# Three pairs of 128-row TensorE transposes done in 64-row halves, weight loads released by products, and a new order up to the wide gate products

## The chip, the cores and the metric

The kernel runs on one core of a Trainium2 chip. The core has five engines with separate instruction queues: TensorE (PE, matrix products; its weight loads are shown as PEld), VectorE (DVE), ScalarE (ACT), GpSimd (POOL) and SyncE (SP), which here only issues transfers. The metric is the device time of one execution in microseconds (us). Three runs of the kernel before took 202.31, 202.59 and 202.63 us, a median of 202.59.

## What is computed

The input x has 2048 rows of 448 bf16 numbers. Two blocks follow one another, each with a layer norm ahead and a residual sum behind:

```python
qkv = layernorm(x) @ wqkv                       # 16 heads of 28
pq, pk = q @ w_phi, k @ w_phi                   # per head
phi = concat(softmax(p), softmax(-p))           # for p = pq and pk
kv, z = phi_k.T @ v, sum(phi_k)                 # over all 2048 rows
o = (phi_q @ kv) / (phi_q @ z + 1e-6)
h = x + o @ wo
g, u = layernorm(h) @ w_gate, layernorm(h) @ w_up    # 448 -> 1792
out = h + (sigmoid(g) * u) @ w_down
```

## The kernel before, in words

The 2048 rows are 16 tiles of 128 rows, numbered t = 0 to 15, in four chunks of four tiles. A product contracts over the partitions, so each tile must be transposed (features on partitions, rows along the free axis) before it meets a weight. 448 features are held as four blocks of 128 partitions, of which some half blocks are padding; therefore most products are made in pairs of 64 rows: one product uses array rows 0 to 63 and the other rows 64 to 127, at the same time, into two PSUM banks. The helper `both` (L304 to L310) issues such pairs, so nearly all products have line L309. An operation that is split over such pairs has a part "a" and a part "b"; in part "b" the array halves and the banks are swapped, and PE waits between the two for its own part "a".

The stages are these. First x is loaded, normalised (`xn`), and transposed: tiles 0 to 3 by PE against an identity (`pe_transpose`, L533 to L541; the products have line L538 and the copy out of PSUM, `xT0e` and so on, L531), the other twelve tiles by transfers that transpose. For each tile the products `pva`, `pvb` give k and v; ACT makes the two exponentials of k (`ek`, L671 and L672), DVE the row sums and their reciprocals (`ss`, `rs`), DVE or POOL the quotient (`phi`, L685), and PE adds the tile into the 28 by 28 sums of all heads (`kva`, `kvb`, 64 by 58 each). Tiles 0 to 3 are made as `vva`, `vvb` and `ppa`, `ppb`. `w2m1_0` to `w2m1_3` fold `w_phi` into the q weights; `pqa`, `pqb` make q of a chunk, of which ACT takes exponentials (`eq`).

When tile 15 has been added, ACT and DVE bring the sums into `kvz`. Then `num` makes numerators and denominators of a tile, DVE combines them (`rsm`, `qq`, `b`, `c`, `rden`), `o` divides (POOL or DVE, L810), the quotient is transposed (tiles 0 and 1 by PE as `oT0`, `oT1`, the others by transfers), `woa`, `wob` multiply by wo, `h` adds x, and the second layer norm gives `hn`. Tiles 0 and 1 of `hn` are again transposed by PE (`hT0`, `hT1`), the others by transfers. Gate and up products (`ga`, `gb`), the tanh (`sig`, L925), the product (`hh`, L926) and the down products (`dn`, `dp`, `dm`, `dl`) end the work. The gate products of tiles 0 to 3 are 256 wide; those from `ga4_1` on, 512 wide, are the wide gates. They begin at 93.7 us of the span.

The order on every engine is written out: the table `ORDER` names the operations of each engine in sequence, and the name's engine in it also says who does a copy that ACT or DVE could do. The class `Graph` derives the waits from what each operation reads and writes. SP's queue is in order too: a transfer whose data is not ready holds back all that stand behind it. The table `PACE` adds waits that no data needs; before it has one entry, by which `ld_wg1` waits for `kva14`. `wwo` and `wgu` are marks in PE's order at which PE waits for the weights wo, and the gate and up weights, and issues nothing.

## Time and profile before

| what | value |
|---|---|
| median of three runs | 202.59 us |
| the profiled execution | 202.7 us, of which the span is 200.8 us |
| PE busy in the span | 195.5 us (97%), granted clock 1.0 |
| DVE, ACT, POOL busy | 132.0, 89.4, 56.2 us |
| HBM read and written | 8.34 and 1.84 MB |

Times in the views count from the start of the span; 1.9 us of the execution lie outside it. A matmul's shown end is modelled and reaches beyond the start of the next, so the step from one start to the next says what a product costs, and the shown length does not.

### The profile page before, as it was taken

How to read it: one execution, taken by the hardware profiler on the slowest of the kernel's cores; microseconds unless marked ns; L12 is line 12 of the kernel's file. 1: busy time of each engine (PE TensorE's matmuls, PEld its weight loads, DVE VectorE, ACT ScalarE, POOL GpSimd, SP SyncE). 2: the span in 40 equal slices, each digit the busy share in tenths (PEclk: the TensorE clock that was granted, in tenths of full speed). 3: DMA queues.
4: the chain of work that ended last, by engine and by line, in shares of the span. 5: the costliest groups of instructions: out<-in, count | busy, mean ns of one | idle time of the engine just before them, and what ended most of it. 6: DMA issues, size and time to landing. Idle time of an engine off the chain costs nothing.

```text
span 200.8 us, 5854 instructions
## 1 busy us (share of the span) xinstructions
PE 195.5 (97%) x2516; PEld 114.4 (57%) x2516; DVE 132.0 (66%) x308; ACT 89.4 (45%) x174; POOL 56.2 (28%) x95
## 2 busy tenths in 40 slices
PE   7999999999999999999999999999999999999995
PEld 4835556565568778787444444555555555554443
DVE  5999999978888986576569877346332422272224
ACT  2668988898883451434232432324323212222220
POOL 5779948633343207510170110001400000000000
PEclk9999999999999999999999999999999999999999
DMA  6965346749984230360015220020312000004002
GB/s 157 316 140 129 54 83 76 221 144 302 309 206 66 52 57 15 66 82 3 0 29 124 56 42 10 20 58 26 65 38 52 0 3 2 0 3 137 0 3 91
DMA packets 32490, 16.26 MB, mean 81 GB/s; under 512 B 24720, under 2 KB 31568, under 8 KB 32464
## 3 DMA queue, kind: packets, MB, share of 16 engines
q1 hardware_dynamic: 32336, 15.86, 33.7%
q8 instruction: 20, 0.33, 0.7%
q14 instruction: 6, 0.05, 0.1%
q10 hardware_dynamic: 128, 0.03, 0.1%
HBM read 8.34 MB, written 1.84 MB: 51 GB/s over the span
## 4 chain that ended last, share of the span: by engine, by line
PE 92%; ACT 3%; DMA 2%; issue 1%; SPq 1%; DVE 0%
PE psum L309 84%; PE psum L954 5%; DMA wk_sb<-in_A_wqkv_dram 2%; ACT hhT L671 1%; ACT eq L721 1%; ACT hhT L672 1%; PE psum L524 1%; PE psum L538 1%; PE psum L612 1%; SPq L413 1%; PE psum L599 0%; ACT xnT L531 0%; ACT v L531 0%; DVE x_sb L961 0%
## 5 line engine op out<-in xcount | busy, mean ns | idle before, releaser
L309 PE MATMUL psum<-xnT,wu_sb 64*128 64x512 bf16 (+1 forms) x490 | 93.6, 333 | 0.0
L309 PE MATMUL psum<-xnT,wg_sb 64*128 64x512 bf16 (+1 forms) x490 | 93.5, 333 | 0.1
L925 ACT ACTIVATE sg_sb<-psum 128x512 bf16<-128x512 f32 x56 | 33.2, 596 | 90.1 <-PE psum L309 89.5
L926 DVE SCALAR_TENSOR_TENSOR hhT<-sg_sb,psum 128x512 bf16<-128x512 bf16 x56 | 37.7, 684 | 52.1 <-ACT sg_sb L925 51.7
L309 PEld LDWEIGHTS psum<-xnT,wg_sb 64*128 64x128 bf16 x490 | 44.6, 94 | 20.9 <-DVE hhT L926 2.5
L309 PEld LDWEIGHTS psum<-xnT,wu_sb 64*128 64x128 bf16 x490 | 44.7, 94 | 13.9
L309 PE MATMUL psum<-wd_sb,hhT 64*128 64x448 bf16 x336 | 37.3, 349 | 0.0
L309 PEld LDWEIGHTS psum<-wd_sb,hhT 64*128 64x128 bf16 x336 | 17.8, 94 | 14.2 <-DVE x_sb L836 0.5
L309 PE MATMUL psum<-Wk,xnT 64*128 64x448 bf16 x112 | 22.2, 350 | 0.5 <-ACT hhT L672 0.2
L309 PE MATMUL psum<-wv_sb,xnT 64*128 64x448 bf16 x112 | 22.3, 351 | 0.1
L810 POOL TENSOR_TENSOR o_pad<-c_sb,rden 128x448 bf16<-128x448 bf16 x11 | 10.2, 935 | 28.5 <-DVE rden L806 28.4
L675 DVE TENSOR_REDUCE ss<-hhT 128x32 f32<-128x896 bf16 x16 | 16.8, 1060 | 0.2 <-ACT hhT L672 0.2
L721 ACT ACTIVATE eq<-psum 120x1024 bf16<-120x1024 f32 x16 | 15.6, 1030 | 0.6 <-PE psum L309 0.4
L685 POOL TENSOR_TENSOR phi<-hhT,rs 128x896 bf16<-128x896 bf16 x8 | 13.6, 1710 | 5.6 <-DVE rs L681 3.4
L309 PE MATMUL psum<-xnT,Wq 64*120 64x512 bf16 x112 | 14.8, 383 | 0.3 <-ACT eq L721 0.2
L845 POOL TENSOR_SCALAR ve<-ssq 128x1 f32<-128x1 f32 x11 | 2.2, 201 | 41.8 <-ACT junk L842 41.5
L309 PE MATMUL psum<-wo_o,oT 64*128 64x448 bf16 x56 | 13.2, 350 | 0.0
L309 PE MATMUL psum<-wo_e,oT 64*128 64x448 bf16 x56 | 13.2, 349 | 0.0
L961 DVE SCALAR_TENSOR_TENSOR x_sb<-psum,x_sb 128x448 bf16<-128x448 f32 (+2 forms) x17 | 9.4, 592 | 2.9 <-PE psum L954 1.6
L954 PE MATMUL psum<-wd_sb,hhT 128*128 128x448 bf16 (+2 forms) x70 | 11.2, 316 | 0.0
L309 PEld LDWEIGHTS psum<-Wk,xnT 64*128 64x128 bf16 x112 | 7.8, 94 | 5.8 <-PE psum L309 1.0
L671 ACT ACTIVATE hhT<-psum 128x448 bf16<-128x448 f32 x16 | 8.8, 553 | 4.4 <-PE psum L309 4.2
(105 smaller groups left out, 234.4 us busy)
## 6 DMA issues: line engine op xcount, KB each, us to landing
out_dram<-x_sb SPq DMA_DIRECT2D x15, 112.0 KB, 1.8
x_sb<-in_A_x_dram SPq DMA_DIRECT2D x7, 224.0 KB, 4.2
wd_sb<-in_B_w_down_dram SPq DMA_DIRECT2D x7, 224.0 KB, 5.1
wg_sb<-in_B_w_gate_dram SPq DMA_DIRECT2D x3, 448.0 KB, 5.8
wu_sb<-in_B_w_up_dram SPq DMA_DIRECT2D x3, 448.0 KB, 5.7
wv_sb<-in_A_wqkv_dram SPq DMA_DIRECT2D x2, 224.0 KB, 4.7
wk_sb<-in_A_wqkv_dram SPq DMA_DIRECT2D x2, 196.0 KB, 4.1
wo_e<-in_A_wo_dram SPq DMA_DIRECT2D x1, 336.0 KB, 3.3
```

The costliest lines, as they stand in the source:

```text
L309: p = e.matmul(o, lhsT=w, rhs=r, start=st, stop=sp, tile_position=(row, 0))
L413: return op(eng, name, lambda e: e.dma_start(dst, src), r=r, w=w, dma="in" if eng == "sp" else "ain", nring=48 if eng == "sp" else 8, kb=kb)
L671: e.activation(ek[:, s, :, 0, :], src, ACT.Exp)
L675: op("dve", "ss%d" % t, lambda e: e.tensor_reduce(ss[:, s, :].rearrange("p (b h) -> p b h", h=2), eks.rearrange("p b (d h) -> p b h d", h= ...
L685: return e.tensor_tensor(phi[:, sp, :, :, :].rearrange("p b a n -> p (b a) n")[:, :, 0:56].rearrange("p b (d h) -> p b d h", h=2), eks.rea ...
L721: op("act", "eq%d_%d%s" % (c, i, "pm"[sg]), lambda e, sg=sg: e.activation(eq[c][:, sg, 2 * i:2 * i + 2, :].rearrange("p g n -> p (g n)"), ...
L810: return e.tensor_tensor(o_pad[:, t % NO, off:off + D].rearrange("p (h d) -> p h d", h=H), c_sb[:, t % NS, :, 0:DH], rden[:, t % NS, :][:, ...
L845: op(("pool", "dve"), "ve%d" % t, lambda e: e.tensor_scalar(ve2[:, t:t + 1], ssq2[:, t:t + 1], 1.0 / D ** 3, EPS, op0=ALU.mult, op1=ALU.ad ...
L925: op("act", "sig" + nm, lambda e: e.activation(sg_sb[:, k, 0:W], bk(bg)[:, 0:W], ACT.Tanh, scale=0.5), r=[B(bg)], w=[("sg", k)])
L926: op("dve", "hh" + nm, lambda e: e.scalar_tensor_tensor(out=dst, in0=sg_sb[:, k, 0:W].rearrange("p (f n) -> p f n", n=N), scalar=1.0, in1= ...
L954: p = e.matmul(bk(b)[:, lo:hi], lhsT=hb[:, ff, TS(t)], rhs=wd_sb[:, ff, lo:hi], start=ff == 0, stop=ff == FT - 1)
L961: op("dve", "fin%d%s" % (t, nm), lambda e: e.scalar_tensor_tensor(out=h_sb[:, t, lo:hi], in0=bk(b)[:, lo:hi], scalar=0.5, in1=h_sb[:, t, l ...
```

## The change

`pe_transpose` made a tile's transpose as four products over all 128 array rows with 128 columns each. For the pairs xT2/xT3, oT0/oT1 and hT0/hT1 a new function makes both tiles' transposes at once, as 16 products over 64 array rows with 64 columns each; the lower half of the rows of both tiles goes to one PSUM bank and the upper half to the other. There are still two copies out of PSUM for a pair, but each holds one half of the rows of both tiles, so a reader of either tile waits for both copies. xT0 and xT1 stay as they were.

```diff
+        def XT(t):
+            return [("xnT", t, 0), ("xnT", t, 1)]
...
+        def pair_transpose(names, srcs, banks, dst, rkeys, wkeys):
+            ps = [bk16(b)[:, 0:512] for b in banks]
+
+            def f(e):
+                for i, tile in enumerate(srcs):
+                    for kt, src in enumerate(tile):
+                        o = slice((i * KT + kt) * 64, (i * KT + kt + 1) * 64)
+                        for h, rows in enumerate((LO, HI)):
+                            p = e.transpose(ps[h][:, o], src[rows], ident[rows, rows], tile_position=(64 * h, 0))
+                return p
+            op("pe", names[0], f, r=["ident"] + rkeys, w=[B(b) for b in banks], rows=64, half={b: h for h, b in enumerate(banks)})
+            for h in range(2):
+                evac(names[h] + "e", dst[h], ps[h].rearrange("p (t k s) -> p t k s", t=2, k=KT), B(banks[h]), [k[h] for k in wkeys])
...
-            if t < 4:
+            if t in (2, 3):
+                if t == 3:
+                    v = xnT[0][:, :, 2 * P:4 * P].rearrange("p k (t h s) -> p h t k s", t=2, h=2)
+                    pair_transpose(("xT2", "xT3"), [[xn_pad[:, u % NX, kt * P:(kt + 1) * P] for kt in range(KT)] for u in (2, 3)], (6, 7),
+                                   [v[:, 0], v[:, 1]], [("xn", 2 % NX), ("xn", 3 % NX)], [XT(2), XT(3)])
+            elif t < 2:
...
-PACE = {"ld_wg1": "kva14"}
+PACE = {"ld_wg0": "pvb14", "ld_wu0": "pvb15", "ld_wg1": "kvb10", "ld_wu1": "kvb11", "ld_wg2": "kvb12", "ld_wu2": "kvb13", "ld_wg3": "kvb14",
+        "ld_wu3": "pqa1_1", "ld_wd0": "num1", "ld_wd2": "pqb1_1"}
```

`otrans` and `htrans` call the new function in the same way, with banks 2 and 3, and 0 and 1.

The order tables of PE, DVE, ACT and POOL are written anew from xT2 up to about `ga4_1`; behind that, from `num13` on, PE's order is the same word for word. SP's order is unchanged. Between engines these move: `xT3e` from ACT to DVE, `v1_13` from DVE to ACT, `nm1_6`, `nm1_8` and `nm1_12` from ACT to POOL, `phi5` from DVE to POOL and `phi8` from POOL to DVE, `o1`, `o4`, `o10` and `o11` from POOL to DVE, `o7` and `o8` from DVE to POOL, and some small operations of the second layer norm of tiles 2 to 9 both ways. `wgu` moves from among the wide gates to ahead of `num5`, and `wwo` from `kvb14` to behind `pqb1_1`.

The order shows this at three places. On ACT, early in the kernel, between the exponentials of tiles 0 and 1 (L671 and L672 twice) and those of tile 2, the kernel before has:

```order
L455 CAST par<-mask 128x2
L671 ACTIVATE hhT<-psum 128x8x56 [waits s_eng_pe]
L672 ACTIVATE hhT<-psum 128x8x56
L531 COPY xnT<-psum 128x4x128 [waits s_eng_pe]
L671 ACTIVATE hhT<-psum 128x8x56
L672 ACTIVATE hhT<-psum 128x8x56
L531 CAST v<-psum 128x16x28 [waits s_eng_pe]
```

After the change (the same operations stand 1 to 26 lines further down in the file):

```order
L456 CAST par<-mask 128x2
L697 ACTIVATE hhT<-psum 128x8x56 [waits s_eng_pe]
L698 ACTIVATE hhT<-psum 128x8x56
L697 ACTIVATE hhT<-psum 128x8x56
L698 ACTIVATE hhT<-psum 128x8x56
L532 CAST v<-psum 128x16x28 [waits s_eng_pe]
```

The copy of a transposed tile is gone from between the exponentials; it is now a second copy in DVE's queue.

On PE, where the quotients of tiles 0 and 1 are transposed (`o_pad`), between q of chunk 2 and the product with wo, the kernel before has:

```order
L309 MATMUL psum<-xnT,Wq 120x512 [waits s_eng_act]
L309 MATMUL psum<-xnT,Wq 120x512 x7
L538 MATMUL psum<-ident,o_pad 128x128 [waits s_eng_pool,s_eng_dve]
L538 MATMUL psum<-ident,o_pad 128x128 x3
L538 MATMUL psum<-ident,o_pad 128x128 [waits s_eng_pool]
...
L309 MATMUL psum<-kvz,eq 128x60 [waits s_eng_dve]
L309 MATMUL psum<-kvz,eq 128x60 x15
L309 MATMUL psum<-xnT,Wq 120x512 [waits s_eng_pe]
L309 MATMUL psum<-xnT,Wq 120x512 x5
L309 MATMUL psum<-x_sb,ident 128x448 [waits s_eng_dve,s_eng_act]
```

After the change:

```order
L310 MATMUL psum<-xnT,Wq 120x512 [waits s_eng_act]
L310 MATMUL psum<-xnT,Wq 120x512 x7
L548 MATMUL psum<-ident,o_pad 128x64 [waits s_eng_dve,s_eng_pool]
L548 MATMUL psum<-ident,o_pad 128x64 x15
L310 MATMUL psum<-xnT,Wq 120x512 [waits s_eng_pe]
L310 MATMUL psum<-xnT,Wq 120x512 x5
L310 MATMUL psum<-kvz,eq 128x60 [waits s_eng_dve]
L310 MATMUL psum<-kvz,eq 128x60 x15
L310 MATMUL psum<-x_sb,ident 128x448 [waits s_eng_act,s_eng_dve]
```

Two groups of four transposes have become one of sixteen half ones, and the q products (`pqb2_1`) now stand ahead of the 60-column products (`num3`).

On DVE, at the same place, between the numerators of tile 1 and the copy of a transposed quotient out of PSUM, the kernel before has:

```order
L799 TENSOR_TENSOR qq<-rsm,psum 128x16 [waits s_eng_dve]
L801 TENSOR_TENSOR b_sb<-psum,qq 128x464 [waits s_eng_dve]
L804 TENSOR_TENSOR c_sb<-b_sb,psum 128x464 [waits s_eng_dve]
L531 COPY oT<-psum 128x512 [waits s_eng_pe]
L798 RECIPROCAL rsm<-psum 128x16 [waits s_eng_pe]
```

After the change:

```order
L825 TENSOR_TENSOR qq<-rsm,psum 128x16 [waits s_eng_dve]
L836 TENSOR_TENSOR o_pad<-c_sb,rden 128x448 [waits s_eng_dve]
L827 TENSOR_TENSOR b_sb<-psum,qq 128x464 [waits s_eng_dve]
L830 TENSOR_TENSOR c_sb<-b_sb,psum 128x464 [waits s_eng_dve]
L532 COPY oT<-psum 128x8x64 [waits s_eng_pe]
```

The division of tile 1 (`o1`, into `o_pad`) has come into DVE's queue, ahead of tile 2's `b2` and `c2` and of the copy.

34 lines of the change are left out of this document (20 added, 14 removed), and 90 rows, old and new, of the table ORDER.

## The prediction

> **What bounds the kernel now.** I read the busy lines first, then the stretches by stage, then PE's timeline around the three transposes, and last the other engines at the same places.
>
> ```profile
> PE 195.5 (97%) x2516; PEld 114.4 (57%) x2516; DVE 132.0 (66%) x308; ACT 89.4 (45%) x174; POOL 56.2 (28%) x95
> ```
>
> PE is busy nearly all the time, so the end moves only by what leaves PE's queue or by gaps in it. The stretches (length, then busy time of PE, PEld, DVE, ACT, POOL, then granted clock) show where another engine is as full:
>
> ```profile
> 12.00:44.00 32.00, 31.34 (x518) 17.97 (x516) 30.95 (x62) 28.30 (x63) 23.22 (x21) 1.00 0.53 122
> 44.00:59.00 15.00, 14.44 (x255) 8.41 (x249) 12.65 (x37) 13.27 (x19) 5.74 (x7) 1.00 0.97 256
> 59.00:94.00 35.00, 35.00 (x630) 28.40 (x630) 27.21 (x74) 12.65 (x29) 10.31 (x17) 1.00 0.34 58
> 94.00:198.50 104.50, 104.31 (x1012) 52.45 (x1008) 51.65 (x110) 30.11 (x57) 8.98 (x20) 1.00 0.14 34
> ```
>
> From 12 to 44 us DVE is idle 1.05 us of 32, and most of that is one wait at the end: there PE and DVE run neck and neck. From 44 to 59 us a chain of dependent steps leads from the last sum over the rows to the first gate product. Behind 59 us PE has no gap; the order from there on changes only up to 94 us. So the change must earn its time ahead of 59 us, and a saving on PE counts there only where nothing else is late.
>
> PE's timeline at the three places (start, length, what; steps between starts are real, ends are modelled):
>
> ```profile
> 11.23 0.29 PE L524 MATMUL psum<-zero 128*128 128x128 bf16 x2
> 11.35 0.61 PE L538 MATMUL psum<-ident,xn_pad 128*128 128x128 bf16 x8
> 11.89 1.74 PE L309 MATMUL psum<-wv_sb,xnT 64*128 64x448 bf16 x14
> 13.82 1.74 PE L309 MATMUL psum<-Wk,xnT 64*128 64x448 bf16 x14 [0.19 <-ACT hhT L672]
> ...
> 18.02 0.35 PE L309 MATMUL psum<-Wk,xnT 64*128 64x448 bf16 x1 [0.18 <-ACT v L531]
> ...
> 41.34 1.05 PE L309 MATMUL psum<-xnT,Wq 64*120 64x512 bf16 x8
> 42.22 0.39 PE L309 MATMUL psum<-v,phi 64*128 64x58 bf16 x16
> ...
> 49.19 1.07 PE L309 MATMUL psum<-xnT,Wq 64*120 64x512 bf16 x8 [0.25 <-ACT eq L721]
> 50.20 0.62 PE L538 MATMUL psum<-ident,o_pad 128*128 128x128 bf16 x8
> 50.75 0.40 PE L309 MATMUL psum<-kvz,eq 56*128 56x60 bf16 x16
> 50.99 0.84 PE L309 MATMUL psum<-xnT,Wq 64*120 64x512 bf16 x6
> 51.66 0.35 PE L309 MATMUL psum<-x_sb,ident 64*128 64x448 bf16 x2
> ...
> 57.59 0.62 PE L538 MATMUL psum<-ident,hn_pad 128*128 128x128 bf16 x8
> 58.14 0.36 PE L309 MATMUL psum<-wo_e,oT 64*128 64x448 bf16 x1
> 59.01 0.27 PE L309 MATMUL psum<-xnT,wg_sb 64*128 64x256 bf16 x1
> ```
>
> **The transposes on PE.** Eight full transposes take 0.55 us to the next start (50.20 to 50.75; 11.35 to 11.89 and 57.59 to 58.14 likewise). Two warm products of the same 128 columns take 0.12 (11.23 to 11.35), so about 0.07 of the 0.55 is lost at the change from 128-row to 64-row products. Another such loss stands ahead: eight q products take 0.88 (41.34 to 42.22), but 1.01 where transposes follow (49.19 to 50.20), so 0.13. The nearest row for 16 half transposes of 64 columns is the 16 products of 60 columns: 0.24 (50.75 to 50.99). No row shows a half transpose; between 0.24 and 16 times the warm product's 0.06 (0.96) I take 0.24, since rows, columns and pairing are the same. A group then costs PE 0.24 instead of 0.68: 0.44 less at oT, as much at hT, but less at xT, where the warm products ahead keep full rows: 0.54 becomes 0.13 + 0.24 = 0.37, 0.17 less.
>
> [...]
>
> **The front, up to 44 us.** ACT and DVE there:
>
> ```profile
> 12.20 0.59 ACT L531 COPY xnT<-psum 128x512 bf16<-128x512 bf16 x1
> 12.67 0.58 ACT L671 ACTIVATE hhT<-psum 128x448 bf16<-128x448 f32 x1
> 13.10 0.58 ACT L672 ACTIVATE hhT<-psum 128x448 bf16<-128x448 f32 x1
> L531 DVE COPY xnT<-psum 128x512 bf16<-128x512 bf16 x5 | 2.1, 418 | 0.2 <-PE psum L538 0.2
> L531 DVE CAST v<-psum 128x448 bf16<-128x448 f32 x1 | 0.6, 617 | 0.0
> 42.22 1.14 DVE L685 TENSOR_TENSOR phi<-hhT,rs 128x896 bf16<-128x896 bf16 x2
> 44.49 0.81 DVE L750 TENSOR_TENSOR kvz<-psum,mask 64x232 bf16<-64x232 f32 x2 [1.14 <-PE psum L309]
> ```
>
> The copy xT3e leaves ACT: the next exponential starts 0.47 earlier (12.67 - 12.20), and `ppa2`, which waited for it at 13.82, starts at about 13.35, if `vvb0` is through by then: it began its 1.74 at 11.89 and now begins 0.17 earlier. `pva4` at 18.02, which waits for an ACT copy behind the next exponentials, follows by about the same. One fold group (`w2m1_1`) now stands between `ppa2` and `ppb2`, where PE waited anyway. So PE and ACT gain 0.45 early on. DVE takes the copy (0.42) and gives v1_13 away (0.62), 0.20 less by the end of the stage, but 0.42 more until then. Who is last at the end? DVE's last `phi` ends at 43.36 and DVE then idles 1.14 for PE: PE is behind by more than a crossing of halves costs, so PE's gain counts as long as no `phi` comes later than its product. I take 0.45; the ends are 0.20 (only what DVE saves) and 0.80 (PE's gain, and the 0.35 of DVE's idle time beside v1_13). On POOL the three `nm1` and `phi5` for `phi8` come to little; 23.22 busy of 32 hides them. SP's transposing transfers of tiles 4 on wait for POOL's `xn4` behind `nm1_6`, 0.2 later, ahead of products that begin at 18 us.
>
> **oT, 49 to 53.6 us.**
>
> ```profile
> 49.11 0.17 DVE L799 TENSOR_TENSOR qq<-rsm,psum 128x16 f32<-128x16 f32 x1
> 49.31 0.64 DVE L801 TENSOR_TENSOR b_sb<-psum,qq 128x464 bf16<-128x464 f32 x1
> 49.99 0.64 DVE L804 TENSOR_TENSOR c_sb<-b_sb,psum 128x464 bf16<-128x464 bf16 x1
> 50.86 0.42 DVE L531 COPY oT<-psum 128x512 bf16<-128x512 bf16 x1 [0.23 <-PE psum L538]
> L810 DVE TENSOR_TENSOR o_pad<-c_sb,rden 128x448 bf16<-128x448 bf16 x5 | 3.1, 625 | 0.1
> L810 POOL TENSOR_TENSOR o_pad<-c_sb,rden 128x448 bf16<-128x448 bf16 x11 | 10.2, 935 | 28.5 <-DVE rden L806 28.4
> ```
>
> PE saves 0.44, but what it feeds is behind DVE. With `o1` there (0.63, less about 0.08 by which DVE's steps overlap where none waits for the one ahead, as 58.03 + 0.43 and 58.37 below), `b2` starts at 49.86, `c2` at 50.54 and ends at 51.18, and the copy of one half runs from about 51.10 to 51.52. `woa0` follows at about 51.6, against 51.66; PE is ready for it at 51.66 - 0.44 = 51.2 and idles. So of 0.44 only 0.05 arrives; between 0 and 0.44 I take 0.05. POOL is relieved, `o0` alone (0.94) ends in time, and the transfers of oT2 and oT3 behind have until 58.14.
>
> **hT, 53.6 to 59 us.**
>
> ```profile
> 56.83 0.41 DVE L851 TENSOR_SCALAR hn_pad<-x_sb,mv,rst 128x512 bf16<-128x512 bf16 x1
> 58.03 0.43 DVE L531 COPY xnT<-psum 128x512 bf16<-128x512 bf16 x1 [0.15 <-PE psum L538]
> 58.37 0.16 DVE L799 TENSOR_TENSOR qq<-rsm,psum 128x16 f32<-128x16 f32 x1
> 58.44 0.42 DVE L531 COPY xnT<-psum 128x512 bf16<-128x512 bf16 x1
> ```
>
> Again a chain: the second `hn` ends at 57.24 on DVE, and `c4` now stands ahead of both. The transposes can begin at about 57.43 instead of 57.59 and end at 57.67; both copies, 0.8 together, wait for them and for `qq5`, and end at 58.7 instead of 58.86. The first gate product comes at 58.85 instead of 59.01; of these 0.16, 0.05 is oT's, since the chain starts from there, and 0.10 is hT's own out of 0.44. PE idles about 0.4 ahead of it. Bounds 0 and 0.44.
>
> **The weight loads.**
>
> ```profile
> 46.33 0.44 SPq L413 DMA_DIRECT2D wu_sb<-in_B_w_up_dram  x1
> 52.60 2.93 SPq L823 DMA_TRANSPOSE oT<-o_pad  x2
> wu_sb<-in_B_w_up_dram SPq DMA_DIRECT2D x3, 448.0 KB, 5.7
> ```
>
> The last gate or up load was issued at 46.33; now it waits for `pqa1_1`, eight q products (0.88) right behind the last row sums, which DVE's `kvz` follows at 44.49: about 45.4. Those ahead of it go out with the sums of tiles 10 to 14, before nearly all with tile 14. With 5.7 to landing it is there by 51.1, and `wgu` asks shortly before hT's 57.59. SP's oT2 behind the paced loads waits for its quotient until 52.60 anyway. I cost it at nothing; were the cover gone, `num5` and hT would wait for the landing.
>
> **From 59 to 94 us** the same products stand in another order in a stretch without gaps; 0, with 0.2 to either side.
>
> **Sum.** 0.45 + 0.05 + 0.10 = 0.60 off the profiled 202.7 gives 202.1; the median lies 0.11 below that execution, so 202.0.
>
> **The rivals.** *All of PE's savings arrive* (chance 0.13): DVE's order leads `b2` and `c2` in time, and oT and hT count in full: 0.45 + 0.44 + 0.44 = 1.3, 201.3. The idle ahead of `woa0` and of the first gate speaks against it.
>
> *Nothing arrives that can be told* (0.20): DVE's extra 0.42 early on holds the `phi` and with it PE, and only v1_13's 0.20 is won: 202.4.
>
> *The half transposes do not pair* (0.04): 16 steps one after another, each half the warm step, 0.03, make 0.48 a group; the idle at oT and hT hides it, and 0.24 of the front's gain goes: 202.2. The row of 16 in 0.24 speaks against it. [...]
>
> *Slower* (0.19): DVE becomes the bound from 12 to 44 us. xT3e stands ahead of all row sums, v1_13 goes only near the end, and PE now asks earlier. It decides from the point where a `phi` on DVE ends after PE has reached its product: each tile then waits, PE's queue holds the next tile's projections behind it, ACT gets its exponentials later, and DVE in turn its sums. Price: the copy's 0.42 not made up, plus one ACT exponential and its wait exposed where it was the other way (0.47 - 0.42): about 0.45, 203.05. For it speaks DVE's 30.95 of 32; against it the 1.14 of idle at its end.
>
> **Chances and range.** My forecast holds 0.44 (201.6 to 202.5). A change under 0.2%, 0.4 us, can hardly be told from none by measuring this kernel. Faster: 0.36 of the forecast's 0.44, the 0.13, and 0.02 of the 0.04, 0.51. Same: 0.08 + 0.20 + 0.02 = 0.30. Slower: 0.19. The range 201.2 to 202.9 leaves out some 0.11 of the slower case and 0.05 at the fast end.
>
> **What would show it.** One group of 16 transposes should stand at each place with about 0.24 to the next product's earliest start, and 0.1 less ahead. `ppa2` should start near 13.35, DVE's `kvz` wait shrink, the first gate stand near 58.4, and gaps of 0.4 show ahead of `woa0` and of the first gate. I am wrong if DVE's sums run late in the front (a `phi` releasing PE), or if the gate stretch gets gaps.

## The result, and the profile after

The changed kernel takes 203.33 us (median of 19 runs, 202.06 to 205.35), the kernel before beside it 202.41 (19 runs, 202.05 to 202.98). The ratio is 1.0037, with a 95% interval of 1.0023 to 1.0052: slower by 0.4%, where 0.3% faster was forecast. The executions of the changed kernel fall into two groups of about equal size, eight from 202.06 to 202.77 and ten from 203.25 to 204.16 (one more at 205.35), all at a granted clock of 0.999 or 1.0; those of before have one group. Every ratio in this document leaves out executions more than 1.5% above the fastest of their kernel: 205.35 here, two of o7_dve and three of after_merge further down. The profile after is of the first group, at 202.38 with a span of 200.6.

Its busy lines and its stretches, columns as before:

```profile
PE 195.3 (97%) x2540; PEld 112.8 (56%) x2540; DVE 133.3 (66%) x313; ACT 89.4 (45%) x171; POOL 52.6 (26%) x93
```

```profile
12.00:44.00 32.00, 31.69 (x556) 18.16 (x552) 30.31 (x63) 28.53 (x61) 24.00 (x23) 1.00 0.56 135
44.00:59.00 15.00, 14.40 (x254) 8.16 (x248) 13.78 (x39) 13.18 (x18) 3.91 (x5) 1.00 0.78 230
59.00:94.00 35.00, 34.36 (x618) 26.05 (x616) 27.89 (x79) 12.55 (x28) 9.43 (x16) 1.00 0.29 58
94.00:198.50 104.50, 104.12 (x1010) 52.74 (x1006) 52.05 (x108) 29.91 (x57) 7.09 (x18) 1.00 0.16 34
```

PE had no gap from 59 to 94 us before (35.00 of 35.00); now it has 0.64 there. PE's timeline at the three places of the transposes:

```profile
11.01 0.29 PE L525 MATMUL psum<-zero 128*128 128x128 bf16 x2
11.23 0.41 PE L548 MATMUL psum<-ident,xn_pad 64*128 64x64 bf16 x16
11.47 1.73 PE L310 MATMUL psum<-wv_sb,xnT 64*128 64x448 bf16 x14
13.04 0.92 PE L310 MATMUL psum<-Wk,xnT 64*128 64x448 bf16 x8
13.89 0.37 PE L638 MATMUL psum<-Wphi,WqT 112*128 112x112 bf16 x4
14.19 0.74 PE L310 MATMUL psum<-Wk,xnT 64*128 64x448 bf16 x6
...
48.51 1.07 PE L310 MATMUL psum<-xnT,Wq 64*120 64x512 bf16 x8 [0.25 <-ACT eq L747]
49.42 0.40 PE L548 MATMUL psum<-ident,o_pad 64*128 64x64 bf16 x16
49.65 0.85 PE L310 MATMUL psum<-xnT,Wq 64*120 64x512 bf16 x6
50.49 0.40 PE L310 MATMUL psum<-kvz,eq 56*128 56x60 bf16 x16
50.83 0.36 PE L310 MATMUL psum<-x_sb,ident 64*128 64x448 bf16 x2
...
56.76 0.41 PE L548 MATMUL psum<-ident,hn_pad 64*128 64x64 bf16 x16
57.01 0.35 PE L310 MATMUL psum<-wo_e,oT 64*128 64x448 bf16 x1
...
58.02 0.28 PE L310 MATMUL psum<-xnT,wg_sb 64*128 64x256 bf16 x1
```

Each group of halves takes 0.23 to 0.25 to the next start. `ppa2` starts at 13.04 (13.82 before), `woa0` at 50.83 (51.66), and the first gate product at 58.02 (59.01): 0.99 is gained up to there. PE and SP at 70 us then show where most of it is lost:

```profile
69.63 0.27 PE L310 MATMUL psum<-xnT,wu_sb 64*128 64x256 bf16 x1
...
70.54 0.35 PE L310 MATMUL psum<-wo_e,oT 64*128 64x448 bf16 x1 [0.64 <-issue]
```

```profile
66.88 2.43 SPq L851 DMA_TRANSPOSE oT<-o_pad  x1
69.35 1.27 SPq L884 DMA_TRANSPOSE xnT<-hn_pad  x1
```

and the same transfer in the kernel before:

```profile
67.37 1.19 SPq L823 DMA_TRANSPOSE oT<-o_pad  x1
```

The group at 70.54 is `woa6`, which needs the transposed quotients of tiles 6 and 7. The transfer of oT7 was issued 0.5 earlier than before, but its issue took 2.43 instead of 1.19, and it landed at 70.45 (69.79 before). While SP issued it, the trace shows a packet of 16,384 bytes on another queue, q8, kind "instruction", from 67.46 to 68.88. There are 20 such packets in each profile, here that of after (packets, MB, share of the DMA engines):

```profile
q8 instruction: 20, 0.33, 0.7%
```

PE has 5,080 matmuls and weight loads after and 5,032 before, and most of the packets start about 256 of these apart (at counts of 1696, 1960, 2188, 2452 and 2708 after, twice the matmuls begun; the median of the 19 steps is 256 after and 246 before). From this spacing they are taken here for PE's own program, fetched in blocks of about 256 instructions. Three pairs of tiles in halves are 24 matmuls and 24 weight loads more, so every block begins that much earlier in the program than before. The longer "issue" entries of the profiles, waits that they cannot name, are read here as a wait for such a delayed transfer (0.64 at 70.54, behind oT7's landing at 70.45), or as PE waiting for its own block.

The landmarks of the profiles, read from PE's timeline (us from the start of the span). "To gate" is from `ppa2` to the first gate product, "gates" from there to the first wide gate product (`ga4_1`); from that to the last product it is 104.5 in all of them, so `ga4_1` decides the time:

| kernel | ppa2 | first gate | ga4_1 | to gate | gates |
|---|---|---|---|---|---|
| before | 13.82 | 59.01 | 93.70 | 45.19 | 34.69 |
| changed | 13.04 | 58.02 | 93.50 | 44.99 | 35.48 |
| after_again | 13.25 | 59.41 | 94.60 | 46.16 | 35.19 |
| gates_before | 12.85 | 60.93 | 97.52 | 48.08 | 36.59 |
| half_only | 13.67 | 60.22 | 96.44 | 46.55 | 36.22 |
| before_fill49 | 17.64 | 63.62 | 99.80 | 45.98 | 36.18 |
| half_merge | 13.77 | 59.60 | 94.28 | 45.83 | 34.68 |
| after_old_pace | 12.90 | 59.35 | 94.30 | 46.44 | 34.95 |
| woa6_later | 12.98 | 58.52 | 94.63 | 45.54 | 36.11 |
| old_pace_wd_late | 13.14 | 58.74 | 94.00 | 45.60 | 35.26 |
| wd_late_woa6 | 13.08 | 59.73 | 95.97 | 46.64 | 36.24 |
| half_merge_wd_late | 13.90 | 59.01 | 93.87 | 45.11 | 34.86 |
| front_new_gates_old | 12.76 | 57.75 | 93.58 | 44.98 | 35.83 |
| front_new_gates_new | 13.11 | 59.23 | 94.57 | 46.12 | 35.34 |
| front_new_full | 13.36 | 58.86 | 94.35 | 45.51 | 35.49 |
| before_new_pace | 14.11 | 59.33 | 94.01 | 45.22 | 34.68 |
| best | 13.51 | 59.40 | 94.22 | 45.90 | 34.82 |
| w2m_later | 13.23 | 59.71 | 94.55 | 46.48 | 34.84 |

Each row is one profiled execution, and `ppa2` alone varies from 12.85 to 13.25 in the eight rows with the same order and the same warm products up to there; the verdicts below go by the timed runs, and the rows say where the time is. The profiled executions of `o7_dve` and `after_merge` had a granted clock of 0.992 and are not in the table: in both, PE stands long at one place described below (2.11 and 3.34 us), and the granted clock is 0.5 for 3.41 us, from 51.12 and 50.20 on.

### The profile page after: what moved, and what is told of

The parts are those of the page before. It is cut to its first block, busy times and chain, and to the rows that moved or that the text cites. A ratio compares the mean times of both kernels' runs of the same rounds, so it can differ in the third digit from the quotient of the medians.

```text
span 200.6 us, 5898 instructions
## 1 busy us (share of the span) xinstructions
PE 195.3 (97%) x2540; PEld 112.8 (56%) x2540; DVE 133.3 (66%) x313; ACT 89.4 (45%) x171; POOL 52.6 (26%) x93
## 4 chain that ended last, share of the span: by engine, by line
PE 96%; ACT 1%; DVE 1%; issue 1%
PE psum L310 85%; PE psum L984 5%; PE psum L525 2%; PE psum L638 1%; ACT eq L747 1%; PE psum L492 1%; PE psum L625 0%; DVE xnT L532 0%; PE psum L559 0%; PE psum L548 0%; PE psum L486 0%; DVE x_sb L991 0%; DVE zero L418 0%; DVE rsm L824 0%; PE psum L733 0%
## 5 line engine op out<-in xcount | busy, mean ns | idle before, releaser
L836 POOL TENSOR_TENSOR o_pad<-c_sb,rden 128x448 bf16<-128x448 bf16 x9 | 8.4, 938 | 41.7 <-DVE ve L873 22.9
L827 DVE TENSOR_TENSOR b_sb<-psum,qq 128x464 bf16<-128x464 f32 x16 | 10.1, 634 | 0.7 <-PE psum L310 0.4
```

Of the source, the lines that this page charges most:

```text
L827: op("dve", "b%d" % t, lambda e: e.tensor_tensor(h3(b_sb), OMv[:, :, :, 0:EV], h2(qq)[:, :, :, None].to_broadcast([P, NB, 8, EV]), ALU.mul ...
L836: return e.tensor_tensor(o_pad[:, t % NO, off:off + D].rearrange("p (h d) -> p h d", h=H), c_sb[:, t % NS, :, 0:DH], rden[:, t % NS, :][:, ...
```

## The experiments

**First round: which part costs.** The changed kernel again, with nothing edited:

> The changed kernel as it is. Theory 'transfer': the front's gain (first gate product at 58.0 us instead of 59.0) is there in every execution and is lost between 59 and 94 us, where PE waits ahead of a wo product for a transposed quotient that a transfer brings; in an execution of about 203.8 us the first gate still starts near 58.0 and 1.4 us more of such waits show behind it. Theory 'front': in an execution of about 203.8 us the first gate itself starts 1 us late, at 59 or later, because weights or the row sums come late there.

Measured: 203.69 (203.07 to 204.21, 7 runs), ratio 1.0059 (1.0038 to 1.0080). The chain of its profiled execution, of the second group, has three entries that the profile after has not, or not so:

```profile
10.31 4.08 DMA WqT<-in_A_wqkv_dram
...
46.86 0.62 issue
...
71.28 0.35 issue
```

PE waits 0.4 at `w2m1_1` (14.5 us) for the transposed q weights, stands still 0.62 in the middle of `pqb1_1`, six products with nothing between them to wait for, and waits for oT7 again. The first gate product stands at 59.41, as theory 'front' had it (59 or later), and the gates take 35.19, not more than in the profile after (35.48). So this execution loses its time ahead of the gates. Late weights, which theory 'front' had named, are one part of it; the stand in `pqb1_1` no theory had.

The order of before from the first gate product on, on every engine (PE's shown):

```diff
-... ga0_2 ga0_0 ga0_1 num6 ga0_3 gb0_0 ... gb0_10 woa6 num9 wob6 ga0_12 ...
+... ga0_2 ga0_0 ga0_1 num6 gb0_0 ga0_3 ... gb0_9 woa6 ga0_11 wob6 gb0_10 ...
```

> The changed kernel up to woa2, and behind that the order of the kernel before on every engine (o7 back on DVE, o4 on POOL, and so on). Theory 'transfer', if the new order between 59 and 94 us is what loses: no wait ahead of woa6, the 1.0 us of the front arrives, about 201.4 us, and executions within 0.5 us of one another. Theory 'front': the median stays near 203.3, in two groups.

Measured: 205.57 (204.07 to 206.60, 6 runs), ratio 1.0147 (1.0107 to 1.0186). That is above both expectations; the old gate order does not mend it. Its chain shows the same three waits, all longer:

```profile
10.05 4.84 DMA WqT<-in_A_wqkv_dram
...
47.37 1.63 issue
...
72.19 1.61 issue
```

Only the quotient of tile 7 given back to DVE:

```diff
-    pool: ... ve2 o7 ve3 ...    dve: ... rden7 hh0_4 ...
+    pool: ... ve2 ve3 ...       dve: ... rden7 o7 hh0_4 ...
```

> One operation moved back: o7 from POOL to DVE, right behind rden7. Theory 'transfer': the quotient is ready 0.5 us earlier (66.4 instead of 66.85), its transfer is issued 0.4 us earlier, and PE's 0.64 us ahead of woa6 shrinks by as much; 0.4 us faster than the changed kernel, or more where the issue itself is shorter than 2.4 us. Theory 'front': no change, 203.3 in two groups.

Measured: 203.40 (202.39 to 207.33, 9 runs), ratio 1.0050 (1.0018 to 1.0081). No gain can be told; the 0.4 that was expected of it would hardly show among times this far apart.

The halves alone, with the order of before and its single wait for the weight loads:

```diff
-    pe: ... warm9 xT2 xT3 vva0 ... pqa2_1 oT0 oT1 num3 ... num5 hT1 hT0 woa2 ...
+    pe: ... warm9 xT2 vva0 ... pqa2_1 oT0 num3 ... num5 hT0 woa2 ...
```

> The kernel before with its own order and its one paced load; only the three pairs of transposes are made in halves. By the sum on record, without the copy moved off ACT: PE saves 0.17 at xT, and of 0.44 at oT about 0.2 arrives (no o1 on DVE there), of 0.44 at hT about 0.15: 0.2 to 0.5 us faster than before, first gate at 58.5 to 58.8. Theory 'transfer' adds: 48 more PE instructions move the fetches of PE's instruction blocks against SP's transfers, so a wait of up to 1 us ahead of a wo product may appear, and the time lies between 202.0 and 203.2.

Measured: 204.95 (204.24 to 207.16, 6 runs), ratio 1.0134 (1.0096 to 1.0173), the surprise of the round: less work on PE, the order of before, and 2.6 us slower than the kernel before beside it (202.35). Waits of that kind were expected, but a time of 203.2 at most. Its chain has two:

```profile
54.12 5.21 DMA oT<-o_pad
...
71.34 1.36 issue
```

At 59.46 `woa2` has waited 1.7 for oT2 and oT3, and `woa6` then 1.4 for oT7. The transfer of oT2 was issued 0.2 earlier than before and landed 2.0 later. What differs is the fetches. Read from the trace, transposing transfers with the fetch nearest to them:

```
kernel               transfer    issued          block fetched   landed   landing less fetch's end
before               oT7         67.37-68.56     70.92-71.87      69.79   (fetched later)
half_only            oT7         68.58-69.78     70.55-71.54      72.62   1.08
gates_before         oT7         69.42-70.61     71.28-72.67      73.70   1.03
before               oT2         52.60-53.81     50.75-51.91      56.84   (fetched earlier)
half_only            oT2         52.39-53.60     55.09-57.71      58.81   1.10
before               oT5         62.17-63.36     64.36-65.32      66.35   1.03
changed              WqT, last    9.97-11.23     12.72-13.66      12.83   (already through)
gates_before         WqT, last   10.05-11.32     12.89-13.85      14.90   1.05
front_new_gates_new  WqT, last    9.98-11.24     12.66-13.79      14.99   1.20
```

In all 20 profiles together, a fetch begins between the end of the issue and the landing of 73 transfers of oT and WqT. 49 of them land behind the end of the fetch, by a median of 1.09 (0.88 to 1.59), and a median of 3.1 behind the end of their issue, against 1.25 for the 215 with no fetch from issue to landing. The other 24 land within 0.7 of the fetch's start. Where the fetch holds back an issue of such a transfer, that ends 0.42 to 0.45 behind the fetch, up to 2.5 long instead of 1.2. In the kernel before the fetches hit oT5 and hT2, among others, which have time to spare.

**Second round: is it the count of instructions?** Nothing but 49 more instructions in PE's queue of the kernel before, waits that are already satisfied, two to an instruction (`FILL` is 49):

```diff
+                            if o.name == "wsp":
+                                for _ in range(2 * FILL):
+                                    eng.wait_ge(sems[("eng", "dve")], 1)
```

> The kernel before with nothing changed but 49 more PE instructions, semaphore waits that are already satisfied, ahead of the small fill `wsp`, behind five warm products of 512 columns that keep PE's array busy for 2.1 us. PE's queue then has as many instructions as with the halves (5135 against 5086), so every boundary between blocks of 256 instructions falls 49 instructions earlier in the program; transposes, order and released loads are those of before. Theory A (the fetch of a block of PE's instructions, 16,384 bytes on queue q8, delays a transposing transfer that is in flight, by 1 to 2 us, and the halves moved these fetches): the fetches that stood at 50.75 and 58.88 move to about 50 and 55, where the transfers of oT2 and oT3 run, and the one at 70.92 moves to about 70, nearer to oT7's transfer; idle of PE 0.5 to 1.8 ahead of woa2 (58.1) or of woa6 (70.0), 203.3 to 205.5. Rival B (what costs is the order from the gates on, or the halves themselves): 202.35 as before, at most 0.3 more where the added instructions are not hidden, and no new idle at either place.

Measured: 208.55 (208.03 to 210.88, 6 runs), ratio 1.0317 (1.0273 to 1.0360), above the upper end. The added waits were hidden in part only. In the trace they stand 0.106 apart, 49 in 5.2 us, and the product behind them starts at 6.58 instead of 3.28:

```profile
6.58 0.65 PE L489 MATMUL psum<-zero 128*112 128x512 bf16 x1 [3.09 <-POOL nm L557]
```

That is 3.30, which I had put at next to nothing. After this idle PE's products of 112 columns go 0.094 apart (16 in 1.50, from 7.01 on) where eight took 0.44 before (from 7.19 on), until about 10.9 us, and `ppa2` stands at 17.64 instead of 13.82. But behind that the expected waits are there, in a kernel whose transposes, order and loads are those of before:

```profile
62.86 0.35 PE L313 MATMUL psum<-wo_e,oT 64*128 64x448 bf16 x1 [0.71 <-DMA oT<-o_pad]
...
76.07 0.35 PE L313 MATMUL psum<-wo_e,oT 64*128 64x448 bf16 x1 [1.33 <-issue]
```

From `ppa2` to the first gate product it takes 0.79 more than before and in the gates 1.49 more: 2.28 that goes with where the blocks fall. Together with the 3.82 ahead of `ppa2` that is the whole difference of the two profiled spans (206.9 against 200.8).

The opposite: the halves, with 19 warm products fewer of the same total columns, so that the blocks fall nearly where they did before:

```diff
-(4, 512), (1, 512), (1, 128), (2, 128), (1, 128), (6, 128), (4, 128), (6, 128), (8, 128), (2, 128)
+(4, 512), (1, 512), (1, 128), (1, 256), (1, 128), (2, 384), (1, 512), (2, 384), (2, 512), (1, 256)
```

> Order and released load of before, transposes in halves (as in half_only), and the warm products behind the first five merged to fewer and wider ones of the same columns: 19 matmuls and 19 weight loads less, so that PE's queue has 5097 instructions, 11 more than before and 38 fewer than half_only. Theory A: the fetches fall back to nearly where they were, the idle of 1.7 ahead of woa2 and of 1.4 ahead of woa6 goes; what the halves save arrives in part: 201.8 to 202.4. Rival B (the halves or the transfers are late for another reason than the count of instructions): as half_only, 204.5 to 205.3.

Measured: 202.49 (202.24 to 203.27, 10 runs), ratio 0.9994 (0.9978 to 1.0010), 2.5 below half_only. PE's row of its gate stretch is full again in its profile (the slowest of its ten executions):

```profile
59.00:94.00 35.00, 35.00 (x628) 28.36 (x626) 27.05 (x74) 12.41 (x28) 10.32 (x17) 1.00 0.38 65
```

In that profile `woa2` still waits 0.98 for oT2 and oT3, in whose flight no block is fetched; the down loads issued ahead of them land just before (57.66; oT2 58.23, oT3 58.71). With the landings above, these two runs show the count of instructions to be the cause of what half_only lost. They also say that with the old order the halves bring nothing that can be measured.

The changed kernel with the single wait of before for the weight loads:

```diff
-PACE = {"ld_wg0": "pvb14", "ld_wu0": "pvb15", "ld_wg1": "kvb10", ... "ld_wd0": "num1", "ld_wd2": "pqb1_1"}
+PACE = {"ld_wg1": "kva14"}
```

> The changed kernel with one difference: the weight loads wait as in the kernel before (one wait, for kva14) instead of ten. Theory C (the released loads fill the DMA engines from 40 to 52 us, share 1.00 at 42 to 46 against 0.28 before, and the block of PE's instructions that is asked for at about 43 comes 1 to 3 us late, so that PE stands still in the middle of pqb1_1; this is the slower of the two groups of times): the fetch starts at about 42.5, no idle in pqb1_1, no second group of times near 203.8; median 202.0 to 202.5, with the idle ahead of woa6 still there, since the boundaries are the same. Rival D (the released loads help, and the slower group has another cause): as the changed kernel, 203.3 to 203.8, or slower because the weights land later, with idle ahead of the first gate product.

Measured: 203.35 (202.56 to 203.99, 12 runs), ratio 1.0039 (1.0023 to 1.0056): no faster, and the median that was expected was missed by 0.9. But the stand in `pqb1_1` is gone, as the theory said. The stretch of 42 to 46 us (last but one column: share of the DMA engines) is full with the ten waits and was not before. Before, after, and after_old_pace:

```profile
42.00:46.00 4.00, 3.68 (x117) 2.47 (x115) 2.71 (x8) 3.74 (x8) 0.23 (x1) 1.00 0.28 80
```

```profile
42.00:46.00 4.00, 3.77 (x124) 2.59 (x122) 2.24 (x7) 3.96 (x8) 0.00 (x0) 1.00 1.00 319
```

```profile
42.00:46.00 4.00, 3.77 (x137) 2.66 (x134) 2.28 (x6) 3.96 (x8) 0.00 (x0) 1.00 0.57 180
```

The block that starts at the 603rd matmul before, and at the 604th in half_only, then starts late among the weights, at the 630th to 722nd in the profiles with ten waits, and in six of the eight PE then stands at the 722nd to 724th, which is read here as the end of the code that it has. In these profiles (times of the fetch; when PE goes on; how many matmuls it had done):

```
kernel         block fetched   PE goes on   less fetch's end   matmuls done, and in what
changed        43.10-44.26     (no stand)
after_again    44.68-45.94     47.47        1.53               723, in pqb1_1
gates_before   46.43-47.53     49.00        1.47               723, in pqb1_1
before_new_pace  45.43-46.46   48.17        1.71               723, in pqa2_0 (further down)
o7_dve         46.98-48.01     49.70        1.69               723, in pqb1_1
after_merge    48.00-49.28     50.83        1.55               722, in num2
woa6_later     43.73-44.80     (a step of 0.30 where 0.22 is usual)
w2m_later      44.59-45.75     47.30        1.55               724, in pqb1_1
```

It is the same place in the count and three different places in the work, so PE waits for nothing that the work makes. In before_new_pace and w2m_later it is short: steps of 0.48 and 0.42 from one product to the next, where 0.22 is usual. Of the twelve profiles without the ten waits none has this stand, though the block is late in some of them too (front_new_full: at the 674th matmul, with a share of 0.41). That full engines are what delays it is read from the two going together; no run shows it apart. What after_old_pace gained there it lost at `woa2`:

```profile
58.59 0.35 PE L309 MATMUL psum<-wo_e,oT 64*128 64x448 bf16 x1 [1.08 <-DMA oT<-o_pad]
```

The loads now go out together at 43.3 and later, three loads of the down weights stand between them and oT2 and oT3, and a block fetched from 54.98 to 56.89 catches oT2. So the ten waits were worth something there.

The changed kernel with the merged warm products:

```diff
-(4, 512), (1, 512), (1, 128), (2, 128), ...
+(4, 512), (1, 512), (1, 128), (1, 256), ...
```

> The changed kernel with the warm products merged as in half_merge, 38 PE instructions fewer, the rest as changed (ten released loads, the new order). Theory A and C together: the boundary that falls on oT7's transfer moves 38 instructions later in the program, about 1 us behind, so the idle of 0.4 to 0.6 ahead of woa6 goes or moves; the idle in pqb1_1 stays, since the DMA engines are as full, but its boundary stands about 0.7 us later: 202.2 to 203.5. If neither depends on the count of instructions: 203.4 to 203.7.

Measured: a ratio of 1.0062 (1.0018 to 1.0105), with single times from 202.80 to 207.28 in 6 runs. The median is 205.59. That is too wide to tell the cases apart. In its profile PE stands 3.34 at the 722nd matmul and `woa6` still waits 1.09, behind a block fetched from 73.02 to 74.08: the transfers are later there as well.

**Third round: can the single waits be taken away?** `woa6` two groups later:

```diff
-    pe: ... gb0_10 woa6 num9 wob6 ga0_12 ga0_13 gb0_11 ...
+    pe: ... gb0_10 num9 ga0_12 woa6 ga0_13 wob6 gb0_11 ...
```

> The changed kernel with the group woa6 (first of two output products that need oT6 and oT7) moved two groups later on PE, behind num9 and ga0_12, 0.6 us. Theory A (the 0.4 to 0.6 of idle ahead of woa6 is a wait for oT7's transfer, whose issue took 2.4 us while a block of PE's instructions was fetched): that idle falls to 0.1 or less and the end comes 0.3 to 0.6 earlier; the idle in pqb1_1 stays where an execution has it, so times from 201.8 to 203.4, median about 203.0. Rival (PE stands for its own instructions there as well, at the boundary near 2214): the idle stays at the same count of instructions, now ahead of another group, 203.4 to 203.8.

Measured: 203.94 (203.51 to 204.33, 6 runs), ratio 1.0066 (1.0044 to 1.0087). Both expectations missed. oT7 landed at 70.28, in time now, but the group put ahead waits as well:

```profile
70.71 0.40 PE L306 MATMUL psum<-kvz,eq 56*128 56x60 bf16 x16 [0.46 <-DVE c_sb L826]
```

DVE is about as late at 70 us as oT7, so moving one wait away shows the next; the gates take 36.11, 0.63 more than in the profile after.

Single wait, and the down loads behind oT2 and oT3:

```diff
-    sp: ... ld_wu3 ld_wd0 ld_wd1 ld_wd2 oT2 oT3 ld_wd3 ld_wd4 ld_wd5 ld_wd6 oT4 oT5 oT6 ...
+    sp: ... ld_wu3 oT2 oT3 ld_wd0 ld_wd1 ld_wd2 ld_wd3 oT4 oT5 ld_wd4 ld_wd5 ld_wd6 oT6 ...
```

> The changed kernel with the weight loads waiting as before (one wait, kva14) and the loads of the down weights behind the transfers of oT2 and oT3 on SP's queue, with the last three behind oT5, instead of three ahead of oT2 and four ahead of oT4. Theory C (what the single wait costs is that oT2 and oT3 land behind three down loads, 57.9 and 58.5, and woa2 waits 1.1 for them): oT2 and oT3 land before 57.0, no idle ahead of woa2 but the 0.4 of hT's chain, no idle in pqb1_1, one idle of 0.4 to 0.6 left ahead of woa6: 202.2 to 202.6. Rival (the transfers wait for something else than these loads): woa2 still 1 us late, 203.3.

Measured: 203.05 (202.66 to 203.58, 10 runs), ratio 1.0026 (1.0011 to 1.0042). oT2 landed at 55.25 and `woa2` waits 0.36 instead of 1.08, all of it for oT3, caught by a block at 55.08. 0.30 of the expected 0.8 to 1.1 arrived; oT7 landed at 70.95 and the wait ahead of `woa6` is still there.

Both edits together:

```diff
-    pe: ... gb0_10 woa6 num9 ...            sp: ... ld_wu3 ld_wd0 ld_wd1 ld_wd2 oT2 oT3 ...
+    pe: ... gb0_10 num9 ga0_12 woa6 ...     sp: ... ld_wu3 oT2 oT3 ld_wd0 ...
```

> Both together: single wait, down loads behind oT2 and oT3, woa6 two groups later. If theories A and C hold, no idle in pqb1_1, ahead of woa2 or ahead of woa6 beyond 0.1 to 0.4, and the first gate product at about 58.0 to 58.3 against 59.0 before: 201.6 to 202.0, faster than both kernels. If the costs only move to the next transfer (oT4 and oT5 behind the down loads, woa4 at 65): 202.4 to 203.0 with idle ahead of woa4.

Measured: 204.25 (203.34 to 204.85, 10 runs), ratio 1.0071 (1.0052 to 1.0089). The two don't add: its profile has the wait for WqT (`w2m1_1` 1.1 late, fetch 12.78 to 13.67, landed 14.86) and oT6 and oT7 land at 71.47 and 72.19, behind a block fetched from 69.31 to 70.51.

The down loads later in half_merge:

```diff
-    sp: ... ld_wu3 ld_wd0 ld_wd1 ld_wd2 oT2 oT3 ...
+    sp: ... ld_wu3 oT2 oT3 ld_wd0 ...
```

> Order of before, halves, merged warm products (as half_merge, 202.49), with the down loads behind oT2 and oT3 in the same way. Theory C: the wait of woa2 for oT2 and oT3 (0.98 in half_merge's profile) goes; what the halves save at hT and in the front, 0.3 to 0.6, arrives: 201.9 to 202.2. Rival (the halves bring nothing with the old order, since DVE is the bound): 202.4 to 202.6 with the idle ahead of woa2 turned into idle ahead of the first gate product.

Measured: 202.46 (202.20 to 202.75, 10 runs), ratio 0.9991 (0.9978 to 1.0004). The rival's case: `woa2` no longer waits (57.82), and PE waits for the copies ahead of the first gate product instead, which stands at 59.01, as before. In this profile, with the old order, DVE's copies are the bound there (0.27 of wait).

**Fourth round: where the front's gain comes from, and what the new gate order costs.** The new front with halves, the old gates, the single wait, merged warm products, and the last three down loads behind oT7:

```diff
-    sp: ... ld_wu3 ld_wd0 ld_wd1 ld_wd2 oT2 oT3 ld_wd3 ld_wd4 ld_wd5 ld_wd6 oT4 oT5 oT6 oT7 hT2 ...
+    sp: ... ld_wu3 oT2 oT3 ld_wd0 ld_wd1 ld_wd2 ld_wd3 oT4 oT5 oT6 oT7 ld_wd4 ld_wd5 ld_wd6 hT2 ...
```

> The changed kernel's order and halves up to the first gate product, the order of before behind it, the single wait of before for the weight loads, warm products merged (5098 PE instructions, 12 more than before), the down loads behind oT2 and oT3 and the last three behind oT7. From the first gate product to the first product of the second half (ga4_1) the kernel before needs 34.69 and half_merge 34.68, the profile after 35.47. If the new front is worth the 1.0 seen in the profile after and nothing collides: first gate product at 58.0 to 58.4, ga4_1 at 92.7 to 93.1, time 201.4 to 201.9, faster than both. If the front's gain belongs to the ten released loads: first gate product at 58.7 to 59.0, 202.2 to 202.5.

Measured: 202.69 (202.33 to 204.12, 12 runs), ratio 1.0016 (0.9999 to 1.0034). The first gate product stands at 57.75, 1.26 earlier than before, without the ten waits, so they are not what the front's gain needs; it comes with the order and the halves. At 75.55 most of it is gone:

```profile
75.55 0.27 PE L305 MATMUL psum<-xnT,wg_sb 64*128 64x256 bf16 x1 [0.84 <-DMA xnT<-hn_pad]
```

hT2 landed at 75.01 (73.42 before), behind the three down loads that I had put there and a block fetched from 70.51 to 72.19. The miss is of my own making.

The same with the new gate order:

```diff
-    pe: ... gb0_9 woa6 ga0_11 wob6 gb0_10 ...
+    pe: ... gb0_9 gb0_10 woa6 num9 wob6 ga0_12 ...
```

> As front_new_gates_old, but with the changed kernel's order behind the first gate product as well. If that order by itself makes DVE the bound there (num9 waited 0.46 for DVE's c step in woa6_later): 35.2 to 35.6 from the first gate product to ga4_1 with the instruction blocks out of the way, 0.5 to 0.9 slower than front_new_gates_old. If only the collision with oT7 costs there: the same as front_new_gates_old within 0.2.

Measured: 202.91 (202.10 to 204.29, 10 runs), ratio 1.0016 (0.9993 to 1.0040), the same ratio as the old gates, though the intervals would hide 0.4. The table says it more closely: with the new gate order the gates take 34.84 in w2m_later and 34.95 in after_old_pace, against 34.69 before, and PE waits 0.13 and 0.25 at `woa6` there. So the new gate order does not by itself cost the 0.79 of the profile after; the collision does. The times stand in two groups, 202.10 to 202.47 and 203.35 to 204.29. The profile, at 203.45, is of the second, and in it `w2m1_1` waited 1.1 for WqT, about the distance of the groups.

The same front with full transposes and warm products as before:

```diff
-    pe: ... xT2 vva0 ... oT0 pqb2_1 ... hT0 woa2 ...
+    pe: ... xT2 xT3 vva0 ... oT0 oT1 pqb2_1 ... hT1 hT0 woa2 ...
```

> As front_new_gates_old, but with full transposes in place of the halves and the warm products as before (5087 PE instructions, so that the blocks fall where they did before). What the halves bring in the new front by themselves: 0.3 to 0.6 by the steps of the prediction, so 201.9 to 202.3 here. If the halves bring nothing and the order all: the same as front_new_gates_old within 0.15.

Measured: 203.63 (202.90 to 204.57, 8 runs), ratio 1.0058 (1.0038 to 1.0079). From `ppa2` to the first gate product it takes 45.51 against 44.98 with halves: 0.52, within what was expected of the halves. The timed difference, 0.94, is larger; `ppa2` is 0.6 later in its profile, of which the longer transposes explain 0.3 at most (0.55 against 0.24) and the rest may be arrival.

The ten waits in the kernel before:

```diff
-PACE = {"ld_wg1": "kva14"}
+PACE = {"ld_wg0": "pvb14", "ld_wu0": "pvb15", "ld_wg1": "kvb10", ... "ld_wd0": "num1", "ld_wd2": "pqb1_1"}
```

> The kernel before with one difference: the ten waits of the changed kernel for the weight loads in place of one. Theory C: DMA share near 1.0 at 42 to 46 (0.28 before), the block of PE's instructions asked for at about 43.2 starts 0.5 to 3 us late, and where its end lies behind about 45.3 PE stands still at its 1446th instruction (723 matmuls), for as long as the end of the fetch plus 1.5 us is behind the time at which PE got there, 46.9: 202.4 in some executions and 203 to 205 in others. Rival: the block has enough lead in this order, 202.2 to 202.5 in all.

Measured: 202.84 (202.20 to 203.70, 10 runs), ratio 1.0018 (1.0002 to 1.0034). The DMA share of 42 to 46 us is 1.01, and the block comes at 45.43 to 46.46, 2.2 later than before. PE stands for it at its 723rd matmul (a step from 47.69 to 48.17), less than elsewhere, since in this order it gets there later; up to the first gate product that is made up (45.22 from `ppa2`, 45.18 before). The theory holds at that place. Three of the ten times are at 203.29 to 203.70, above all 33 of the kernel before beside it (203.19 at most), but no gap parts them from the rest: a second group made by this alone is not shown.

**Last round.** front_new_gates_old with `w2m1_1` back behind `vvb2` and the down loads spread two, three and two:

```diff
-    pe: ... ppa2 w2m1_1 ppb2 vva2 vvb2 seed w2m1_3 ...      act: ... ek2 w2e1_1 v1_2 ...
+    pe: ... ppa2 ppb2 vva2 vvb2 seed w2m1_1 w2m1_3 ...      act: ... ek2 v1_2 w2e1_1 ...
-    sp: ... ld_wu3 oT2 oT3 ld_wd0 ld_wd1 ld_wd2 ld_wd3 oT4 oT5 oT6 oT7 ld_wd4 ld_wd5 ld_wd6 hT2 ...
+    sp: ... ld_wu3 ld_wd0 ld_wd1 oT2 oT3 ld_wd2 ld_wd3 ld_wd4 oT4 oT5 ld_wd5 ld_wd6 oT6 oT7 hT2 ...
```

> front_new_gates_old with two repairs. The fold group w2m1_1, which waited up to 1.4 for WqT in some executions, stands behind vvb2 and the seed again instead of between ppa2 and ppb2; and the last two down loads stand between oT5 and oT6 instead of three behind oT7, where they made hT2 land at 75.0 and PE wait 1.0 for it at 75.5 (two down loads go ahead of oT2, three behind oT3). The first gate product stood at 57.75 in front_new_gates_old and 59.01 before. If these two waits are what was left, 1.0 to 1.2 of it arrives: ga4_1 at 92.5 to 92.8 against 93.70, time 201.2 to 201.7 in one group, faster than both kernels. If the wait for hT2 has another cause (the block of instructions fetched at 70.5 alone) or the down loads catch oT6 and oT7: 202.0 to 202.6.

Measured: 202.58 (202.29 to 203.56, 12 runs), ratio 1.0009 (0.9993 to 1.0024), where 201.2 to 201.7 was expected if these two waits were all. The gates take 34.82, so the wait for hT2 is gone. But the fold group at its new place makes a wait of its own, since the next one needs a bank that ACT has yet to empty:

```profile
16.93 0.37 PE L633 MATMUL psum<-Wphi,WqT 112*128 112x112 bf16 x4
17.98 0.57 PE L633 MATMUL psum<-Wphi,WqT 112*128 112x112 bf16 x8 [0.69 <-ACT Wq L650]
```

From `ppa2` to `pva4` it takes 4.97, against 4.19 in front_new_gates_old. The combination of front_new_gates_old with only the loads' repair, which by these rows would have its first gate product at 57.75 and the gates in 34.8, was not run.

The changed kernel with the same move of the fold group only:

```diff
-    pe: ... ppa2 w2m1_1 ppb2 ...      act: ... ek2 w2e1_1 v1_2 ...
+    pe: ... seed w2m1_1 w2m1_3 ...    act: ... ek2 v1_2 w2e1_1 ...
```

> The changed kernel with one difference: the fold group w2m1_1 behind vvb2 and the seed, as before, instead of between ppa2 and ppb2 (its cast on ACT one step later). If the slower of the two groups of times is an execution in which a fetched block of PE's instructions catches the last WqT transfer, which then lands 1.0 to 1.2 behind the end of the fetch, at 14.4 to 15.0 instead of 12.8: one group, 202.0 to 202.6. If the slower group is the late block at PE's 1446th instruction (the stand in pqb1_1): both groups as in the changed kernel, median 203.3 to 203.7. If both: the share of executions above 203 falls, but not to none.

Measured: 203.39 (202.90 to 205.05, 8 runs), ratio 1.0052 (1.0030 to 1.0074). Seven of the eight lie within 0.74, and none is near 202.4, but the same new wait, which costs 0.8 in best, stands in the profile (17.71, 0.69 on ACT), and `woa2` waits 0.74 behind a block fetched from 55.89 to 57.26. WqT landed at 15.05, caught by a block at 13.05 to 14.01, and PE did not wait for it. That agrees with WqT as a maker of the two groups; with a new wait of its own it does not prove it.

## Why the prediction was wrong

- **The halves on PE.** Right: 16 in 0.24, 0.23 and 0.25 where 0.24 was forecast. They pair, as the 16 numerator products do (0.24 before); the 0.48 of the rival without pairing is not borne out. The eight q products ahead of oT take 0.91 (48.51 to 49.42) instead of 1.01, so the loss of 0.13 at the crossing went to 0.03.
- **The front, 0.45.** Too small: `ppa2` is 0.78 earlier, not 0.47, and the last row sums (`kvb15`) 0.68 earlier. PE is through `vvb0` at 13.04 and no longer waits for ACT there; some 0.2 of the 0.78 stood already at the warm products (11.01 against 11.23); before, PE had waited 0.23 and 0.16 for `wk_sb` by then, after it did not. DVE's idle ahead of `kvz`, the cover named, was forecast to shrink and is 1.23 (1.14 before).
- **oT, 0.05, and hT, 0.10.** Right in kind: the shares of 0.44 that arrived are 0.15 each. Of the idle that was forecast, 0.4 at each place, about 0.25 stands ahead of the first gate product and 0.1 ahead of `woa0`. `b2` and `c2` did move behind `o1`, by 0.5 against the last row sums, but the copy of the halves, which had waited 0.23 for PE before, ends only 0.17 later.
- **"From 59 to 94 us ... 0, with 0.2 to either side"** is the step that failed in the first group. The gates take 35.48 instead of 34.69, 0.64 of it by the wait of `woa6` for oT7, which a fetched block of PE's instructions caught. The new order itself does not cost it (34.84 and 34.95 in w2m_later and after_old_pace, where `woa6` waits 0.13 and 0.25). Of 0.99 gained, 0.20 is left, and 202.38 is what that execution took. That the first group lies as near to the forecast of 202.0 as it does is luck: more was gained ahead of the gates than the 0.60, and most of it was lost behind.
- **"One fold group (`w2m1_1`) now stands between `ppa2` and `ppb2`, where PE waited anyway"** failed in part of the executions. Of the ten profiles with that order at a granted clock of 1.0, WqT's last transfer landed at 12.83 to 13.23 in the four in which no block caught one of WqT's, and at 13.79 to 14.99 in the six others; of these six, four waited 0.4 to 1.3 at `w2m1_1`. The prediction looked at PE's idle and not at what the moved group asks for.
- **The weight loads, "I cost it at nothing"**, failed in another part. The landing was in time, as forecast (51.76 for a use at 56.35). What had no term is that the block which PE needs at its 723rd matmul starts late while the weights fill the DMA engines (a share of 1.00 from 42 to 46 us, 0.28 before). after_again shows 0.6 of stand, gates_before with the same front 1.6, o7_dve 2.1.
- **The missing term** is common to the last three: 48 more PE instructions move every block, and what decided in these runs is which transfer each fetch then hit. before_fill49 shows 2.28 of it in the kernel before, for 49, nearly four times the 0.60 that was forecast for the whole change. The prediction counted instructions by their time only.
- **The rivals.** The slower one, DVE the bound from 12 to 44 us, did not come (DVE 30.31 of 32, and still idle at the end); slower came by a way that was not among them. How much of the second group is WqT and how much the stand at the 723rd matmul stays open: after_again's profile has 0.4 of the one and 0.8 of the other (`num0` to `pqa2_0` 1.95 instead of 1.13).

## What to carry to other kernels

In a kernel whose waits are tuned to a few tenths of a us, count the instructions that a change adds to a long queue, and look in the trace where the packets of kind "instruction" fall against the transfers that someone waits for; a change that saves work can lose more by moving them (half_only lost 2.6 us). Two controls told it here: add the same number of idle instructions to the old kernel (and read it behind them, since they cost time of their own, 3.30 here), and take as many away from the new one. When a group is moved earlier, ask when its operands land in the worst execution, not whether the engine was idle at that place.
